# Linear attention in tiles of 64 rows by two positions, ahead of a top-2 mixture of experts, on one core

## The chip, the cores and the metric

One core of one Trainium2 chip. The metric is device time in microseconds (us), the median of several executions; lower is better. One further execution was recorded by the hardware profiler, and all rows come from it.

## What is computed

Three stages in fp32: a linear attention with a norm, a mixture of experts in which every token goes to 2 of 8 experts, and an MLP. Cut to what matters:

```python
# q, k, v: (4, 8, 576, 64)
kv = np.einsum('bhsd,bhse->bhde', k, v)
out = np.einsum('bhsd,bhde->bhse', q, kv)
x = out / sqrt(mean(out * out, -1) + 1e-6) * g_norm      # to (2304, 512)
noisy = x @ w_gate + log1p(exp(x @ w_noise)) * noise     # 8 experts
# the two largest, softmax over the two: top2, top2_w
x[t] = sum over the two e of top2_w * (relu(x[t] @ w1[e]) @ w2[e])   # 512 -> 1024 -> 512
g = s * relu(x @ w_in) ** 2 + b                          # 512 -> 2048
result = g @ w_out
```

## The kernel before, in words

The work has a front (lines 204 to 759) and a main part. The front computes the attention, the norm, the gating logits and the table that says which tokens go to which expert. The main part (from line 762) runs the experts and the MLP as a long row of matmuls (`l1`, lines 789 to 803; `l2`, lines 816 to 827), in the order written out by hand in `steps`. Engines run their instructions in program order, so a wait of one instruction holds everything behind it on that engine.

**Loads.** SyncE issues all loads of q, k and v. `load_batch` (L227) brings the first 512 of a batch's 576 positions as 128 rows of 4 positions for each of 8 heads (pieces of 1 KB), and the last 64 positions separately (`kr`, `vr`, `qr`, pieces of 256 B). Batches 0 and 1 are requested at the start, k and v of batch 2 after `kv(0)`, later ones in the loop.

**K'V.** `kv(b)` (L331) accumulates k'v of a batch: 40 fp32 matmuls with 64-column weights, 32 over 128 rows and 8 over the 64 remaining rows. An fp32 matmul stands as two records in the trace, a transpose as one. ScalarE evicts it to `kvc` and to the block-diagonal weights `kvbd`. `mfold_a` and `mfold_b` fold the gate weights in, so that one attention matmul gives output and logits.

**Token loop** (L728 to L756). There are 18 tiles of 128 tokens (`TILES`, L68): for two batches four tiles each of one position of 128 rows, and a ninth of both batches' last 64 rows. For each tile: VectorE (GpSimd from tile 10) copies q together (`repack`, L381); TensorE transposes it four times (`q_tr`, L395) and ScalarE evicts `qT`; four matmuls of 160 columns (`att`, L404; L414 for the ninth tile, in half-width weights); ScalarE evicts x (L421) and squares it (L425); VectorE copies the logits (L423) and sums the squares (L429); the inverse root goes through ScalarE (L438, L439), GpSimd (L441 to L443) and VectorE (L450); GpSimd scales the logits (L452); VectorE scales x (L461) and sums the logits (L462, `lg`); SyncE stores x to `xs` in DRAM (L467). `kv(1)` to `kv(3)` stand in the loop by `KV_AT`, their folds by `FA`, `FB`.

**Gating chain.** When the first 9 tiles have their logits, `gating(0)` (L582) starts. It is a generator that is advanced by `tick()` calls, five a tile, placed between the norm's instructions. It selects the experts (L498 to L510), ranks tokens with matmuls (L542), builds one-hots (L522, nine instructions), gets the row table of the first 256 tokens of expert 0 (`idx_e`), gathers their rows from `xs` (L186), and at its 34th tick transposes them (`put_x`, L370: L373 TensorE, L376 ScalarE, L377 VectorE). From tile 12 on `advance` splits four weight units in high and low parts (L145, L152 ScalarE, L147 VectorE, L153 GpSimd). The first expert matmul (L801) follows the last tile's attention and `put_x` on TensorE.

**End.** `finish` evicts the MLP's tiles and stores each to the rows that `out_rows` gives: one DMA of 128 rows, two for the ninth and eighteenth tile.

Of the kernel before, what the change touches and what calls it, by code (L numbers as in the profile page):

```python
# [21 lines left out]
def kernel(  # L22
# [25 lines left out]
    NP = H // 2  # L48
    NJ = 4
    SM = P * NJ  # L50
    SR = S - SM
# [13 lines left out]
    PW = 2 * HW_  # L65
# [3 lines left out]
    for b0 in range(0, B, 2):  # L69
        for b in (b0, b0 + 1):  # L70
            TILES += [(b, j) for j in range(NJ)]
        TILES.append((b0, b0 + 1, None))

    def out_rows(t):
        if len(TILES[t]) == 2:
            b, j = TILES[t]
            return [(0, P, out[b * S:b * S + SM].rearrange("(p j) d -> p j d", j=NJ)[:, j, :])]
        b0, b1, _ = TILES[t]
        return [(0, SR, out[b0 * S + SM:(b0 + 1) * S]), (SR, P, out[b1 * S + SM:(b1 + 1) * S])]
# [143 lines left out]
    def load_rest(b):  # L223
        for nm, src in (("kr", k), ("vr", v)):
            nc.sync.dma_start(KQV[b, nm], src[b, :, SM:].rearrange("h p d -> p h d"))

    def load_batch(b, what):  # L227
        def main_rows(t, src, h0, h1):
            nc.sync.dma_start(t[:, h0:h1].rearrange("p h j d -> p h (j d)"),
                              src[b, h0:h1, :SM].rearrange("h (p j) d -> p h (j d)", j=NJ))  # L230

        if what == "kv":
            for nm, src in (("k", k), ("v", v)):
                KQV[b, nm] = pool.tile([P, H, NJ, D], F32, name=nm, bufs=2)
                KQV[b, nm + "r"] = pool.tile([SR, H, D], F32, name=nm + "r", bufs=2)
            for i, (h0, h1) in enumerate(((0, H // 2), (H // 2, H)) if b == 0 else ((0, H),)):
                for nm, src in (("k", k), ("v", v)):
                    main_rows(KQV[b, nm], src, h0, h1)
                if i == 0:
                    load_rest(b)  # L240
            return
        KQV[b, "q"] = pool.tile([P, H, NJ, D], F32, name="q", bufs=2)
        for h0, h1 in ((0, H // 2), (H // 2, H)) if b == 0 else ((0, H),):
            main_rows(KQV[b, "q"], q, h0, h1)
        if b % 2 == 0:
            KQV[b // 2, "qr"] = pool.tile([P, H, D], F32, name="qr", bufs=2)
        o = SR * (b % 2)
        nc.sync.dma_start(KQV[b // 2, "qr"][o:o + SR], q[b, :, SM:].rearrange("h p d -> p h d"))

    nc.scalar.preload_act_table_set("natural_log_exp_and_others")  # L250
    for b in range(2):
        load_batch(b, "kv")
        load_batch(b, "q")
# [4 lines left out]
    def warm(n):  # L258
        ps = small_ps([P, NP, P])
        for _ in range(n):  # L260
            nc.tensor.matmul(ps, lhsT=onesb, rhs=onesb[:, None, :].to_broadcast([P, NP, P]), start=True, stop=True)
# [5 lines left out]
    gw_raw = pool.tile([P, NP, W2C], F32, name="gw_raw")  # L267
    for i, w in enumerate((w_gate, w_noise)):
        for s in range(2):
            gq.dma_start(gw_raw[s * D:(s + 1) * D, :, i * E:(i + 1) * E],  # L270
                         w.rearrange("(s n d) e -> s d n e", s=2, d=D)[s])
# [4 lines left out]
    for s in range(2):  # L276
        r = slice(s * D, (s + 1) * D)
        nc.vector.tensor_scalar(gw[r, :, s], gw_raw[r].rearrange("p (a i) c -> p a i c", a=2), gcol[r], None, op0=OP.mult)
    kvbd = []
    for b in range(B):  # L280
        t = pool.tile([P, NP, PW], F32, name=f"kvbd{b}")
        nc.gpsimd.memset(t, 0.0)
        kvbd.append(t)
    nz = gp.tile([P, NT, E], F32, name="nz")
    TB = 2 * NJ + 1
    for i in range(B // 2):
        nc.gpsimd.dma_start(nz[:, i * TB:i * TB + 2 * NJ, :].rearrange("p (b j) e -> p b (j e)", b=2),
                          noise[2 * i * S:2 * (i + 1) * S, :].rearrange("(b s) e -> b s e", b=2)[:, :SM, :]
                          .rearrange("b (p j) e -> p b (j e)", j=NJ))
    for i in range(2):  # L290
        nc.gpsimd.dma_start(nz[i * SR:(i + 1) * SR, 2 * NJ::TB, :],
                          noise.rearrange("(g b s) e -> b s g e", b=2, s=S)[i, SM:, :, :])
# [38 lines left out]
    def kv(b, h0=0, h1=H):  # L331
        K, V, KR, VR = (KQV[b, n] for n in ("k", "v", "kr", "vr"))
        ps = KVP[b] = KVP.get(b) or small_ps([P, NP, D])

        for j in range(NJ + 1):
            for h in range(h0, h1):
                hp, i = divmod(h, 2)
                lh, rh = (K[:, h, j, :], V[:, h, j, :]) if j < NJ else (KR[:, h, :], VR[:, h, :])
                nc.tensor.matmul(ps[i * D:(i + 1) * D, hp, :], lhsT=lh, rhs=rh, start=j == 0 and h - h0 < 2,
                                 stop=j == NJ and h >= h1 - 2, skip_group_check=True)  # L340
# [105 lines left out]
    def inv_end(t):  # L446
        if t < 0:
            return
# [279 lines left out]
    for t in range(NT + 1):  # L728
# [7 lines left out]
        if t:  # L736
            inv_rms(t - 1)
# [362 lines left out]
```

## Time and profile before, and how to read them

| | us |
|---|---|
| median of 3 executions | 985.84 |
| lowest, highest | 984.59, 987.8 |
| the profiled execution's own time | 983.76 |
| its span in the trace | 982.0 |
| TensorE busy (share of the span) | 942.6 (96%) |
| VectorE busy | 529.9 (54%) |
| ScalarE busy | 397.8 (41%) |
| GpSimd busy | 140.3 (14%) |

PE is TensorE's matmuls, PEld its weight loads, DVE VectorE, ACT ScalarE, POOL GpSimd, SP SyncE; a "q" behind a name is that engine's queue, where DMAs are issued. A share is an average over the whole span; what one stage is worth is read from that stage.

### The profile page before, as it was taken

To read this page: it belongs to the slowest core of one execution; us is meant where nothing else is said; L and a number is where in the kernel's file an instruction comes from. 1 tells how busy PE (TensorE), PEld (TensorE's weight loads), DVE (VectorE), ACT (ScalarE), POOL (GpSimd) and SP (SyncE) were. 2 spreads that over 40 slices of the span, in tenths; PEclk is the share of its full clock that TensorE was granted. 3 is DMA by queue.
4 is the path that set the end of the run, shared out by engine and by line. 5 is a ranking of instruction groups with operands and counts; after the bars stand their busy time and mean duration, and the time that the engine had idled before them with its cause. 6 is when DMAs were issued, how large, how long until landed. Compare 5 with 4: busy or idle time off the path is not lost.

```text
span 982.0 us, 13843 instructions
## 1 busy us (share of the span) xinstructions
PE 942.6 (96%) x5274; PEld 818.5 (83%) x5275; DVE 529.9 (54%) x979; ACT 397.8 (41%) x726; POOL 140.3 (14%) x197
## 2 busy tenths in 40 slices
PE   7866999999999999999999999999999999999998
PEld 5765878989999999999999999788788878887886
DVE  1677785544776666757546456443444443434333
ACT  2765334334554655646435443222222322222221
POOL 3566325010000100100000121100010020000000
PEclk7987999999999999999999999999999999999999
DMA  9965758445484784764645541200120020001001
GB/s 253 282 210 183 231 180 257 149 136 191 151 271 155 247 278 154 238 204 166 206 147 185 172 149 46 65 1 11 32 86 1 22 88 20 0 1 43 1 1 43
DMA packets 111849, 129.00 MB, mean 131 GB/s; under 512 B 14208, under 2 KB 80768, under 8 KB 111776
## 3 DMA queue, kind: packets, MB, share of 16 engines
q1 hardware_dynamic: 104320, 108.03, 34.2%
q0 software_dynamic: 6208, 20.00, 6.9%
q8 instruction: 42, 0.69, 0.3%
q14 instruction: 31, 0.25, 0.1%
q10 hardware_dynamic: 1248, 0.03, 0.1%
HBM read 92.91 MB, written 35.13 MB: 130 GB/s over the span
## 4 chain that ended last, share of the span: by engine, by line
PE 77%; DVE 1%; ACT 1%; issue 0%; ACTq 0%
PE ph L802 13%; PE ph L803 13%; PE ph L801 13%; PE y L825 12%; PE y L826 12%; PE y L827 12%; PE sps L373 2%; DVE r L811 0%; DVE xl L377 0%; ACT hh L813 0%; ACT r L810 0%; DVE r L812 0%; DVE hl L814 0%; DVE rows L834 0%; ACT xh L376 0%
## 5 line engine op out<-in xcount | busy, mean ns | idle before, releaser
L802 PE MATMUL ph<-xl,w1h 128*128 128x320 f32 (+3 forms) x832 | 278.4, 335 | 3.5 <-DVE xl L377 3.5
L801 PE MATMUL ph<-xh,w1h 128*128 128x320 f32 (+3 forms) x832 | 277.9, 334 | 1.5 <-DVEq L882 0.8
L803 PE MATMUL ph<-xh,w1l 128*128 128x320 f32 (+3 forms) x832 | 277.6, 334 | 0.0
L825 PE MATMUL y<-w2h,hh 128*128 128x512 f32 x608 | 243.0, 400 | 0.8 <-PEq L882 0.8
L827 PE MATMUL y<-w2h,hl 128*128 128x512 f32 x608 | 238.4, 392 | 1.0 <-DVE hl L806 1.0
L826 PE MATMUL y<-w2l,hh 128*128 128x512 f32 x608 | 238.3, 392 | 0.0
L802 PEld LDWEIGHTS ph<-xl,w1h 128*128 128x128 f32 x832 | 157.9, 190 | 19.3 <-DVE xl L377 5.9
L801 PEld LDWEIGHTS ph<-xh,w1h 128*128 128x128 f32 x832 | 158.0, 190 | 17.6 <-ACT xh L376 2.3
L803 PEld LDWEIGHTS ph<-xh,w1l 128*128 128x128 f32 x832 | 157.9, 190 | 9.8
L805 ACT ACTIVATE hh<-ph 128x320 fp32r<-128x320 f32 (+2 forms) x128 | 55.9, 437 | 227.0 <-PE ph L803 227.0
L811 DVE SCALAR_TENSOR_TENSOR r<-ph,r 128x512 f32<-128x512 f32 (+1 forms) x80 | 51.0, 638 | 175.9 <-ACT r L810 175.6
L806 DVE SCALAR_TENSOR_TENSOR hl<-ph,hh 128x320 fp32r<-128x320 f32 (+2 forms) x128 | 62.4, 489 | 141.5 <-ACT hh L805 141.5
L827 PEld LDWEIGHTS y<-w2h,hl 128*128 128x128 f32 x608 | 114.4, 188 | 26.4 <-DVE hl L806 1.5
L825 PEld LDWEIGHTS y<-w2h,hh 128*128 128x128 f32 x608 | 114.7, 189 | 21.9 <-ACT xh L376 1.1
L826 PEld LDWEIGHTS y<-w2l,hh 128*128 128x128 f32 x608 | 114.7, 189 | 20.3
L810 ACT ACTIVATE r<-ph 128x512 f32<-128x512 f32 (+1 forms) x80 | 44.4, 554 | 187.8 <-PE ph L803 187.8
L813 ACT ACTIVATE hh<-r 128x512 fp32r<-128x512 f32 (+1 forms) x80 | 47.1, 589 | 101.5 <-DVE r L812 101.5
L186 POOL DMA_INDIRECT rows<-xs,idx x35 | 34.8, 996 | 314.1 <-PE sps L373 183.6
L814 DVE TENSOR_TENSOR hl<-r,hh 128x512 fp32r<-128x512 f32 (+1 forms) x80 | 51.1, 639 | 52.5 <-ACT hh L813 52.5
L186 POOL DMA_INDIRECT rows<-ys,slot_i x36 | 34.5, 959 | 268.3 <-DVE rows L783 133.0
L147 DVE SCALAR_TENSOR_TENSOR w1l<-raw,gcol,w1h 128x512 fp32r<-128x512 f32 x64 | 50.7, 793 | 22.3 <-ACT w1h L145 17.6
L152 ACT ACTIVATE w2h<-raw 128x512 fp32r<-128x512 f32 x80 | 49.7, 621 | 1.5 <-DMA raw<-in_moe_w_dram 1.2
(170 smaller groups left out, 838.9 us busy)
## 6 DMA issues: line engine op xcount, KB each, us to landing
raw<-in_moe_w_dram SPq DMA_DIRECT2D x128, 256.0 KB, 3.7
ys<-rows SPq DMA_DIRECT2D x40, 256.0 KB, 3.7
c_raw<-in_moe_w_in_dram SPq DMA_DIRECT2D x16, 512.0 KB, 6.1
c_raw<-in_moe_w_out_dram SPq DMA_DIRECT2D x16, 512.0 KB, 7.9
wd<-c_fl SPq DMA_DIRECT2D x16, 512.0 KB, 4.8
raw<-wd SPq DMA_DIRECT2D x32, 256.0 KB, 2.9
ys<-zero SPq DMA_DIRECT2D x13, 512.0 KB, 5.5
xs<-x SPq DMA_DIRECT2D x18, 256.0 KB, 5.0
```

Source lines behind the costliest of these rows:

```text
L147: nc.vector.scalar_tensor_tensor(l1.rearrange(fl), r1.rearrange(fl), gcol, h1.bitcast(F32).rearrange(fl), op0=OP.mult, op1=OP.subtract)
L186: nc.gpsimd.indirect_dma_start(out=dst, out_offset=None, in_=src, in_offset=bass.IndirectOffsetOnAxis(ap=icol, axis=0))
L801: nc.tensor.matmul(ps[:, :wd], lhsT=w1h[:, c, :], rhs=xh[:, c, cs], start=c == 0, stop=False)
L802: nc.tensor.matmul(ps[:, :wd], lhsT=w1h[:, c, :], rhs=xl[:, c, cs], start=False, stop=False)
L803: nc.tensor.matmul(ps[:, :wd], lhsT=w1l[:, c, :], rhs=xh[:, c, cs], start=False, stop=c == KC - 1)
L805: nc.scalar.activation(hh[:, cs], ps[:, :wd], AF.Relu)
L806: nc.vector.scalar_tensor_tensor(hl[:, cs], ps[:, :wd], 0.0, hh[:, cs].bitcast(F32), op0=OP.max, op1=OP.subtract)
L811: nc.vector.scalar_tensor_tensor(r[:, :wd], ps[:, :wd], 0.0, r[:, :wd], op0=OP.max, op1=OP.mult)
L814: nc.vector.tensor_sub(hl[:, cs], r[:, :wd], hh[:, cs].bitcast(F32))
L825: nc.tensor.matmul(y, lhsT=hh[:, cs], rhs=w2h, start=f == 0, stop=False)
L826: nc.tensor.matmul(y, lhsT=hh[:, cs], rhs=w2l, start=False, stop=False)
L827: nc.tensor.matmul(y, lhsT=hl[:, cs], rhs=w2h, start=False, stop=f == nf - 1)
```

## The change

Tiles become 64 rows (`HP`) by two positions (`NJ` = 9 positions a row): tile i of a batch is positions 2i and 2i+1 for the same 64 rows, and the ninth tile holds position 8 of both batches. The last 64 positions are no longer special.

- **Loads**: q, k and v of a batch are read flat, as 4 blocks `m` of 128 rows with 576 floats each (pieces of 2304 B). Rows 0 to 63 of block m are head 2m, rows 64 to 127 head 2m+1. q has three buffers.
- **kv**: K is 64 rows and 64 columns, so each matmul uses a quarter of the array: 9 positions x 4 blocks x 2 heads = 72 matmuls a batch, into two accumulators. ScalarE evicts one half of `kvc`, VectorE the other; the block-diagonal copies are split likewise (`kv_diag`, `mfold_b`). `kv(1)`, `kv(2)`, `kv(3)` stand whole behind tile 2, 6 and 11.
- **q_tr**: no repacking; 8 plain matmuls with the identity, 64-column weights straight from q, two tiles ahead. `qT` of odd tiles is evicted by VectorE.
- **att**: 8 matmuls with 64-column weights and 160 columns.
- **Norm**: two tiles a step (`CHUNKS`). One eviction of all 640 columns a tile by ScalarE; squares, sums, Ln, Exp and the scaling are done for both tiles at once; what GpSimd did of it goes to VectorE. One store for two tiles.
- **Noise**: two loads and six copies on GpSimd in place of four loads.
- **Output**: every tile is stored by two DMAs of 64 rows.

The ticks become nine for two tiles; the 34th falls behind the last tile's attention, in the norm of tiles 15 and 16.

```diff
-    NP = H // 2
-    NJ = 4
-    SM = P * NJ
-    SR = S - SM
+    HP = P // 2
+    NJ = S // HP
+    NM = H // 2
...
-            TILES += [(b, j) for j in range(NJ)]
-        TILES.append((b0, b0 + 1, None))
+            TILES += [((b, j), (b, j + 1)) for j in range(0, NJ - 1, 2)]
+        TILES.append(((b0, NJ - 1), (b0 + 1, NJ - 1)))
...
+    def load(b, nm, m0=0, m1=NM):
+        src = {"q": q, "k": k, "v": v}[nm][b].rearrange("h s d -> (h s d)").rearrange("(m r x) -> r m x", r=P, x=NJ * D)
+        if m0 == 0:
+            KQV[b, nm] = pool.tile([P, NM, NJ, D], F32, name=nm, bufs=3 if nm == "q" else 2)
+        nc.sync.dma_start(KQV[b, nm].rearrange("p m j d -> p m (j d)")[:, m0:m1], src[:, m0:m1])
...
+        for j in range(NJ):
+            for a in range(a0, a1):
+                for m in range(2):
+                    for i in range(2):
+                        r = slice(i * HP, (i + 1) * HP)
+                        nc.tensor.matmul(ps[i][m * D:(m + 1) * D, a, :], lhsT=K[r, 2 * a + m, j, :], rhs=V[r, 2 * a + m, j, :],
+                                         start=j == 0 and a == a0, stop=j == NJ - 1 and a == a1 - 1, skip_group_check=True)
+        if a1 == 2:
+            KVP[b] = kvc = pool.tile([P, 2, 2, D], F32, name="kvc", bufs=1)
+            nc.scalar.activation(kvc[:, :, 0], ps[0], AF.Copy)
+            nc.vector.tensor_copy(kvc[:, :, 1], ps[1])
...
+    def q_tr(t):
+        pt = small_ps([P, 2, 2, P])
+        for i, (b, j) in enumerate(TILES[t]):
+            for a in range(2):
+                for m in range(2):
+                    nc.tensor.matmul(pt[m * D:(m + 1) * D, i, a, :], lhsT=KQV[b, "q"][:, 2 * a + m, j, :], rhs=ident,
+                                     start=True, stop=True)
+        qT = pool.tile([P, 2, 2, P], F32, name="qT", bufs=3)
+        if t % 2:
+            nc.vector.tensor_copy(qT, pt)
...
+    def squares(c):
+        x, = XC[c]
+        n = CHUNKS[c][1]
+        sq = pool.tile([P, 2, H, D], F32, name="sq", bufs=1)
+        nc.scalar.activation(sq[:, :n], x[:, :n, :, :D], AF.Square)
...
+        nc.vector.tensor_reduce(ss[:, :n], sq[:, :n], axis=AX, op=OP.add)
...
+    def norm(c):
...
+        nc.vector.tensor_scalar(ss, ss, -0.5 / D, -0.5e-6, op0=OP.mult, op1=OP.add)
+        nc.vector.tensor_mul(u, y, y)
+        tick()
+        nc.vector.tensor_mul(u, u, ss)
+        nc.vector.scalar_tensor_tensor(y, u, 1.5, y, op0=OP.add, op1=OP.mult)
+        tick()
+        nc.vector.tensor_mul(x[:, :, :, D:], x[:, :, :, D:], y[:, :, :, None].to_broadcast([P, n, H, W2C]))
+        tick()
+        nc.vector.tensor_reduce(lg[:, t0:t0 + n, :], x[:, :, :, D:].rearrange("p n h c -> p n c h"), axis=AX, op=OP.add)
+        tick()
+        xn = pool.tile([P, 2, H, D], F32, name="xn", bufs=3)[:, :n]
+        nc.vector.tensor_mul(xn, x[:, :, :, :D], y[:, :, :, None].to_broadcast([P, n, H, D]))
+        tick()
...
+    KV_AT = {2: 1, 6: 2, 11: 3}
+    LOADS = {3: (3, "kv"), 8: (3, "q")}
+
+    for c, (t0, n) in enumerate(CHUNKS):
+        for i in range(n):
+            t = t0 + i
+            att(t)
+            if t - 1 in KV_AT:
+                mfold_a(KV_AT[t - 1])
+            if t + 2 < NT:
+                q_tr(t + 2)
+            if t - 1 in KV_AT:
+                mfold_b(KV_AT[t - 1])
+            if c and i == 0:
+                inv_rms(c - 1)
+            evict(c, i)
+            if t in KV_AT:
+                kv(KV_AT[t])
+            if t in LOADS:
+                b, nms = LOADS[t]
+                for nm in nms:
+                    load(b, nm)
+            if c and i == n - 1:
+                norm(c - 1)
+            if 12 <= t < 16:
+                advance(t - 11)
+            elif t == 11:
+                advance(0)
+        if c and CHUNKS[c - 1][0] + CHUNKS[c - 1][1] == NT0:
             chain[:] = [gating(0), 0]
+        squares(c)
+        put_rows()
```

## Rows read from the trace of the kernel before

**Rows 1.** Timeline, TensorE: start us, us, engine, line, instruction; first expert matmul.

```profile
87.83 0.58 PE L801 MATMUL ph<-xh,w1h 128*128 128x256 f32 x1
```

**Rows 2.** Busy time of TensorE by stretches from 87.83 to 982, their sum.

```profile
sum 894.17, PE 880.09; mean PE 73.34
```

**Rows 3.** Busy us (x) of PE, PEld, DVE, ACT, POOL; PEclk, DMA share, GB/s.

```profile
30.00:40.00 10.00, 6.80 (x76) 6.14 (x77) 8.70 (x23) 7.60 (x21) 5.70 (x13) 1.00 1.14 285
...
60.00:70.00 10.00, 4.50 (x31) 4.33 (x30) 9.62 (x26) 4.42 (x12) 6.81 (x13) 0.77 0.49 166
...
80.00:90.00 10.00, 5.83 (x29) 4.59 (x30) 8.18 (x17) 6.00 (x13) 7.60 (x15) 0.50 0.71 221
```

**Rows 4.** The same view in stretches of 2 us during the loads.

```profile
20.00:22.00 2.00, 2.00 (x9) 1.85 (x8) 0.00 (x0) 0.98 (x3) 0.00 (x0) 0.50 1.10 350
...
22.00:24.00 2.00, 2.00 (x10) 1.96 (x10) 0.29 (x1) 0.92 (x2) 0.00 (x0) 0.50 1.27 212
```

**Rows 5.** Timeline, VectorE: waits for q, first normalization; [idle before <-releaser].

```profile
17.50 1.10 DVE L387 COPY qc<-q 128x512 f32<-128x512 f32 x3 [5.78 <-DMA q<-in_q_dram]
...
30.06 0.43 DVE L387 COPY qc<-q 128x512 f32<-128x512 f32 x1 [5.03 <-DMA q<-in_q_dram]
...
31.38 0.69 DVE L461 TENSOR_TENSOR x<-x,iv 128x512 f32<-128x512 f32 x1
```

**Rows 6.** Timeline, TensorE: K'V, attention of tile 0, quarter weights, half-width attention.

```profile
12.88 1.98 PE L339 MATMUL sps<-v,k 128*64 128x64 f32 x32 [0.76 <-DMA v<-in_v_dram]
...
20.56 2.45 PE L410 MATMUL att<-kvbd,qT 128*128 128x160 f32 x8
...
39.88 0.31 PEld L339 LDWEIGHTS sps<-vr,kr 64*64 64x64 f32 x8
...
45.73 1.31 PE L414 MATMUL att<-kvbd,qT 128*64 128x160 f32 x16
```

**Rows 7.** Groups by shape, 0 to 200 us: count | busy us, mean ns | idle before.

```profile
L429 DVE TENSOR_REDUCE ss<-sq 128x8 f32<-128x512 f32 x18 | 12.2, 677 | 1.4 <-ACT sq L425 1.4
...
L461 DVE TENSOR_TENSOR x<-x,iv 128x512 f32<-128x512 f32 x18 | 12.4, 688 | 0.4
...
L462 DVE TENSOR_REDUCE lg<-raw 128x16 f32<-128x128 f32 x18 | 6.6, 367 | 6.2 <-POOL raw L452 6.2
...
L450 DVE SCALAR_TENSOR_TENSOR iv<-iu,iv 128x8 f32<-128x8 f32 x18 | 3.0, 164 | 4.5 <-POOL iu L443 4.5
...
L498 DVE TENSOR_REDUCE m_all<-g 128x9 f32<-128x72 f32 x4 | 0.9, 229 | 1.4 <-POOL g L485 1.3
...
L834 DVE COPY rows<-y 128x512 f32<-128x512 f32 x2 | 1.4, 682 | 0.0
...
L421 ACT ACTIVATE x<-att 128x512 f32<-128x512 f32 x18 | 10.5, 582 | 3.5 <-PE att L410 3.5
...
L425 ACT ACTIVATE sq<-x 128x512 f32<-128x512 f32 x18 | 11.3, 630 | 0.6
...
L438 ACT ACTIVATE iv<-ss,eps 128x8 f32<-128x8 f32 x18 | 5.4, 299 | 13.0 <-DVE iv L450 10.5 <-DVE ss L429 2.3
...
L145 ACT ACTIVATE w1h<-raw,gcol 128x512 fp32r<-128x512 f32 x21 | 15.1, 717 | 9.2 <-DMA raw<-in_moe_w_dram 9.0
```

**Rows 8.** Timeline, second half of the front, all engines.

```profile
55.05 0.26 ACT L481 ACTIVATE g<-lg 128x72 f32<-128x72 f32 x1 [0.24 <-DVE lg L462]
...
68.36 3.61 DVE L522 TENSOR_SCALAR ohe<-io,early 128x256 f16<-128x256 f16 x9
...
72.77 0.74 DVE L147 SCALAR_TENSOR_TENSOR w1l<-raw,gcol,w1h 128x512 fp32r<-128x512 f32 x1
...
78.50 1.25 POOL L186 DMA_INDIRECT rows<-xs,idx_e  x1 [0.75 <-DVE iv L450]
...
83.60 1.97 PE L373 MATMUL sps<-ident,rows 128*128 128x128 f32 x8 [3.63 <-DMA rows<-xs,idx_e]
```

**Rows 9.** Timeline, SyncE's queue at the end of the kernel.

```profile
977.90 1.11 SPq L842 DMA_DIRECT2D out_dram<-rows  x2
```

More of the change, by code (lines that the diff above doesn't have):

```diff
@@ L221 @@
     KQV = {}
[L223 to L248, printed above, removed]
-    nc.scalar.preload_act_table_set("natural_log_exp_and_others")
-    for b in range(2):
-        load_batch(b, "kv")
-        load_batch(b, "q")
+    def load(b, nm, m0=0, m1=NM):
[3 more added lines that the diff above has]
+        nc.sync.dma_start(KQV[b, nm].rearrange("p m j d -> p m (j d)")[:, m0:m1], src[:, m0:m1])
+    nc.scalar.preload_act_table_set("natural_log_exp_and_others")
+    for m0 in range(0, NM, NM // 2):
+        for nm in "kv":
+            load(0, nm, m0, m0 + NM // 2)
+    load(0, "q")
+    for nm in "kvq":
+        load(1, nm)
     onesb = gp.tile([P, P], BF16, name="onesb")
@@ L258, in warm @@
     def warm(n):
-        ps = small_ps([P, NP, P])
+        ps = small_ps([P, KC, P])
         for _ in range(n):
-            nc.tensor.matmul(ps, lhsT=onesb, rhs=onesb[:, None, :].to_broadcast([P, NP, P]), start=True, stop=True)
+            nc.tensor.matmul(ps, lhsT=onesb, rhs=onesb[:, None, :].to_broadcast([P, KC, P]), start=True, stop=True)
     warm(14)
@@ L266 @@
     gq = nc.scalar
-    gw_raw = pool.tile([P, NP, W2C], F32, name="gw_raw")
+    gw_raw = pool.tile([P, NM, W2C], F32, name="gw_raw")
     for i, w in enumerate((w_gate, w_noise)):
-        for s in range(2):
-            gq.dma_start(gw_raw[s * D:(s + 1) * D, :, i * E:(i + 1) * E],
-                         w.rearrange("(s n d) e -> s d n e", s=2, d=D)[s])
+        gq.dma_start(gw_raw[:, :, i * E:(i + 1) * E], w.rearrange("(m r) e -> r m e", r=P))
     for i in range(2):
@@ L402, in q_tr @@
         QT[t] = qT
     def att(t):
-        tl = TILES[t]
         qT = QT.pop(t)
-        ps = fps.tile([P, NP, 256], F32, name="att", bufs=2)
-        for hp in range(NP):
-            if len(tl) == 2:
-                nc.tensor.matmul(ps[:, hp, :PW], lhsT=qT[:, hp, :], rhs=kvbd[tl[0]][:, hp, :], start=True, stop=True)
-            else:
-                for i in range(2):
-                    r = slice(i * SR, (i + 1) * SR)
-                    nc.tensor.matmul(ps[r, hp, :PW], lhsT=qT[:, hp, r], rhs=kvbd[tl[i]][:, hp, :],
-                                     start=True, stop=True)
@@ L465, in put_rows @@
-    def put_rows():
-        t, x = XO.pop(0)
-        nc.sync.dma_start(xs[t * P:(t + 1) * P, :], x)
+        ps = fps.tile([P, 2, 512], F32, name="att", bufs=2)
+        pv = ps[:, :, :H // 2 * HW_].rearrange("p a (m i c) -> p a m i c", m=2, i=2)
+        for a in range(2):
+            for i in range(2):
+                for s_, (b, _) in enumerate(TILES[t]):
+                    r = slice(s_ * HP, (s_ + 1) * HP)
+                    nc.tensor.matmul(pv[r, a, :, i, :], lhsT=qT[:, s_, a, i * HP:(i + 1) * HP], rhs=kvbd[b][:, a, i],
+                                     start=True, stop=True)
@@ L470, with put_rows @@
+    def put_rows():
+        if not XO:
+            return
+        t, n, x = XO.pop(0)
+        nc.sync.dma_start(xs[t * P:(t + n) * P, :].rearrange("(n p) d -> p n d", n=n), x.rearrange("p n h d -> p n (h d)"))
     GT = {}
```

206 lines of the change are left out of this document (71 added, 135 removed).

## The prediction

> **What bounds the kernel now.** I first looked for the point from which TensorE doesn't rest. The timeline shows the first expert matmul at 87.83 us [rows 1]; from there to the end TensorE is busy 880.09 of 894.17 us [rows 2]. The change leaves that part alone except for the last stores. So the time is the start of that matmul plus a nearly fixed 894 us, and only the front, 0 to 88 us, has to be worked out. 1 us there is 1 us of the result.
>
> In the front I read busy time by stretches [rows 3]. From 30 to 40 us VectorE is the fullest engine (8.70 of 10 us), from 60 to 70 it is full (9.62) while TensorE has 4.50, and TensorE runs at the lower of its two clocks (0.50, 1.2 GHz) from 80 to 90. The DMA share is 1.14 at 285 GB/s in the loading time. There the rate swings between 350 and 212 GB/s in stretches of 2 us with the share never under 1.1 [rows 4]: the engines are always occupied, and the slow stretches are those in which the 256 B pieces of the last 64 positions come. VectorE waits twice for q, 5.78 and 5.03 us [rows 5]. So the front is bound by loads to 30 us, then by VectorE together with what holds it up: waits for GpSimd of 6.2 us before the logit sums and 4.5 us before the roots [rows 7].
>
> **The loads.** 14.2 MB come in pieces of 2304 B instead of 1 KB and 256 B. I take 350 GB/s, the better row [rows 4]; the bounds are 285 [rows 3] and no loss. Batch 0's k and v (2.36 MB) then land at 12.4 us instead of before the matmul at 12.88 [rows 6]; q of batch 1, 4.72 MB later, at 12.4 + 13.5 = 25.9, where before it held VectorE to 30.06 [rows 5]: 4 us earlier.
>
> **K'V.** 72 matmuls instead of 40 a batch, 144 records instead of 80. At the low clock 32 records took 1.98 us [rows 6], 62 ns each, so 31 ns at full clock: 144 x 31 = 4.5 us. If the four quarters overlap fully it is half, 2.2. The eight records on quarter weights took 0.31 us [rows 6], 39 ns each, which is no gain by size and 5.6 us for 144. Bounds 2.2 and 5.6, and I take 3.7, the side of the rows. For batch 0 only the second half (72 records) follows the last landing, at the low clock: 72 x 62 ns = 4.4 us against 2.5 for 40 records. Counting 0.5 us earlier landing, 1.9 us more K'V, and q already there (it came at 17.50 [rows 5], by my reckoning 1.2 us after TensorE could have used it), the first attention matmul is at about 20.8 instead of 20.56 [rows 6]. What lies ahead of it stays: GpSimd's six noise copies push its constants, and VectorE's that hang on them, back by some 4 us, to about 15, hidden by K'V's end at 16.8. Uncovered they would cost up to 4.
>
> **TensorE's tile.** Sixteen half-width records of 160 columns took 1.31 us [rows 6]: that is att, 1.1 us pitch without its tail. q_tr is 16 records of 128 columns, 0.9. Together 2.0 a tile: by themselves no bound.
>
> **VectorE's step of two tiles.** Removed: repacking, the logit copies, half of the instruction starts. Added: evicting qT of the odd tile (0.68, as L834), three small instructions from GpSimd and the logit scaling. From 72 to 512 columns a sum grows from 229 to 677 ns, 1.0 ns a column [rows 7], so 1024 columns cost 1.2. A step is then 0.68 + 1.2 (sums of squares) + 4 x 0.16 + 0.42 (logits) + 0.50 (their sums) + 1.2 (x) = 4.7 us, and its norm alone 2.8. ScalarE: 0.6 (qT) + 2 x 0.7 (eviction, 640 columns) + 1.05 (squares) + 0.6 (Ln, Exp) = 3.6 [rows 7]. Instructions alone, this is no slower than 31.38 to 55.05 us now [rows 5, 8], 2.6 us a tile.
>
> **The wait that is added.** `kv(b)`, its folds and their copies stand between a step's first and second tile, and VectorE now takes part in them. In its order the kvc copy, the diagonal copy, qT and the folded weights come ahead of the norm of the step before. So that norm waits for TensorE: K'V 3.7, then att 1.1, fold 0.4, q_tr 0.9, fold 0.55, copy 0.25: 3.2 more. Queued behind it are norm, sums, then Ln on ScalarE, the eviction, the next attention.
> - First time: att(0) at 20.8, four more pieces of 1.0 to 1.1 to 25.9, q_tr(4) to 26.8 (q has landed), kv(1) to 30.5, norm(0) at 33.7 instead of 31.38. Norm 2.8, sums 1.2, Ln and Exp 0.6: norm(1) 38.3 to 41.1, sums to 42.3.
> - Second: eviction of tile 4 by 39.0, att(6) and q_tr(8) to 41.0, kv(2) to 44.7, norm(2) at 47.9; sums to 51.9, norm(3) 52.5 to 55.3, tile 8's sums to 56.0. The first 9 tiles' logits are there at about 58, against 55.05 [rows 8].
> - Third: sums of tiles 9, 10 end at 60.9; tile 9's eviction at 57.3, att(11), q_tr(13) to 59.3, kv(3) to 63.0, norm(5) at 66.2: about 4 us in which VectorE has little to do.
>
> **The gating half.** norm(5) 2.8 + twelve selections of 0.23 + a weight low part 0.74 + sums 1.2 = 7.5: 73.7. Then `advance(2)` puts a low part ahead of norm(6); it waits for Ln, Exp, an eviction and the high part on ScalarE (0.6 + 0.7 + 0.72 = 2.0), then 0.74 + 2.8 + 0.5 (ranks) + 3.6 (one-hots) + 0.74 + 1.2: 85.3. Again 2.0 + 0.74 and 0.14 for `idx_e`: 88.2. From the gather to the transposes of the gathered rows takes 5.1 us (78.50 to 83.60 [rows 8]): 93.3. Transposes at the low clock 2.0, the eviction 0.6: first expert matmul at 95.9, 8.1 us later than now [rows 1]. What VectorE still owes after it (about 5 us) is as much as before, so no gain or loss there.
>
> **The end.** Three more stores among the last four tiles; two stores of one tile take 1.11 us in the queue [rows 9], one every 0.5 us. They wait mostly for evictions: 0.2, bounds 0 and 1.5.
>
> **Sum.** +8.1 + 0.2 = +8.3 us on the profiled execution's 983.76, which lies 2.1 under the median. Carried over to the median: 985.84 + 8.3, about 994.
>
> **Rivals.**
> - *Quarters side by side.* With 2.2 us a K'V the three norms behind it start 1.5 us earlier each (4.5), batch 0's half 2.2 us: 994 - 6.7 = 987.4, no change that can be told. For it: different rows and columns of the array share nothing. Against: quarter weights show 39 ns a record, not 16 [rows 6]. The Trainium skill, TensorEngine Tiling (Array Packing), Key Properties, says that tiles operate independently and load weights and multiply in parallel, and counts four of them in the 64x64 mode; that is this rival, and no run here shows four. Chance 0.17.
> - *Faster: the waits go and nothing takes their place.* Its place is VectorE's queue. The 4.1 us of earlier q (30.06 to 25.9) come through whole, and the waits for GpSimd, 6.2 and 4.5 us [rows 7], vanish, less about 4 us of added work: 4.1 + 6.7 = 10.8 at most, 975; with half of it handed on, 980.5. It decides if norm(0) starts before about 30 us, that is, if TensorE gets through K'V and folds while VectorE still has sums to do. For it: the full DMA share [rows 3]. Against: the order of the instructions. Chance 0.23.
> - *Low clock in the loop.* If TensorE is granted 1.2 GHz there as at 80 to 90 us [rows 3], K'V and what follows cost 3 to 4 us more each time: 994 + 9 = 1003. Chance 0.08, as TensorE is fuller than before in the first half.
> - The change does not do what it says: it does it in every tile; left out.
>
> **How the numbers follow.** The forecast has 0.52. About 0.3% (3 us) is what a measurement of this kernel can tell from no change. Slower: 0.52 and 0.08, with a little of the forecast's spread (K'V at 2.9, one-hots without GpSimd beside them at 2.2) in the middle: 0.59. Same 0.18, faster 0.23. The forecast's own range is 988 to 999. The range asked for reaches down into the faster rival, 981 to 999.
>
> **What would show it.** Right: k and v of batch 0 land at 12 to 12.5 us with DMA near 350 GB/s; K'V of 144 records near 3.7 us; VectorE idle before norm at about 28 to 33, 43 to 47 and 61 to 66 us, released by TensorE; first L801 record near 96; 894 us behind it. Wrong: VectorE over 9 tenths busy from 30 us on, or the first expert matmul before 85 us; K'V near 2.2 us makes the first rival right; a PEclk of 0.5 between 30 and 65 us the third.

## The result and the profile after

The changed kernel takes 994.98 us in the median of 4 runs (993.61 to 997.58), the kernel before 985.53 on the same chip (4 runs; the 985.84 of the table is the median of three of them): a ratio of 1.0096, 95% interval [1.0069, 1.0123]. The profiled execution took 993.61 us with a span of 991.9, 9.85 us more than the one before.

TensorE's timeline of the changed kernel (start us, us, engine, line, instruction, [idle before <-releaser]) answers to [rows 1, 6]:

```profile
10.96 2.05 PE L322 MATMUL sps<-v,k 64*64 64x64 f32 x72 [1.90 <-DMA v<-in_v_dram]
...
18.56 1.25 PE L397 MATMUL att<-kvbd,qT 128*64 128x160 f32 x16
...
24.19 1.09 PE L380 MATMUL sps<-ident,q 128*64 128x128 f32 x16 [0.46 <-DMA q<-in_q_dram]
...
25.22 2.33 PE L322 MATMUL sps<-v,k 64*64 64x64 f32 x144
...
31.96 0.55 PE L354 MATMUL sps<-gw,kvT 128*128 128x64 f32 x4 [1.78 <-issue]
...
40.42 2.33 PE L322 MATMUL sps<-v,k 64*64 64x64 f32 x144
...
58.77 2.40 PE L322 MATMUL sps<-v,k 64*64 64x64 f32 x144
...
95.32 0.58 PE L789 MATMUL ph<-xh,w1h 128*128 128x256 f32 x1 [0.69 <-ACT xh L370]
```

The first attention matmul comes 2.0 us earlier than before, q of tile 4 (batch 1) has landed at 24.2, and a K'V product of 144 records takes 2.33 to 2.40 us. All of that is better than before or than forecast, and yet the first expert matmul comes at 95.32, 7.5 us later than in [rows 1]. Behind it the row of matmuls is nearly what it was [rows 2]; here is its sum, and the last stores in SyncE's queue [rows 9]:

```profile
sum 896.58, PE 881.43; mean PE 881.43
...
983.95 4.96 SPq L830 DMA_DIRECT2D out_dram<-rows  x8
```

896.58 us in place of 894.17. From the first of the last stores to the end of the span it is now 991.9 - 983.95 = 7.95 us; before, that store was issued at 975.74, 6.26 us from the end. So of the 9.9 us of span 7.5 arose in the front, 1.7 at the end and 0.7 in between.

Stretches of the front: busy us (count) of PE, PEld, DVE, ACT, POOL; PEclk, DMA share, GB/s, as in [rows 3, 4]:

```profile
20.00:30.00 10.00, 9.54 (x256) 8.55 (x252) 2.49 (x4) 5.40 (x11) 0.00 (x0) 1.00 1.06 391
...
30.00:40.00 10.00, 6.56 (x99) 6.22 (x97) 7.32 (x18) 5.22 (x9) 0.00 (x0) 1.00 0.93 345
...
60.00:70.00 10.00, 8.53 (x178) 7.54 (x169) 6.29 (x22) 5.54 (x12) 1.42 (x2) 1.00 0.34 107
...
80.00:90.00 10.00, 5.50 (x44) 3.95 (x44) 8.60 (x17) 3.89 (x7) 2.96 (x3) 0.50 0.46 154
```

From 20 to 30 us the loads run at 391 GB/s, above the better row of before (350), and TensorE is full at its upper clock. VectorE, which was full from 60 to 70 [rows 3], now has 6.29 of 10 us there, and GpSimd has nearly nothing to do. So VectorE, the engine that was short of time, now has time to spare there, and yet the front ends later. Its timeline shows where it waits:

```profile
27.64 0.29 DVE L327 COPY kvc<-sps 128x128 f32<-128x128 f32 x1 [2.77 <-PE sps L322]
...
28.03 0.29 DVE L337 COPY kvbd<-kvc 64x256 f32<-64x256 f32 x1
...
30.22 0.69 DVE L384 COPY qT<-sps 128x512 f32<-128x512 f32 x1 [1.90 <-PE sps L380]
...
32.79 0.23 DVE L360 COPY kvbd<-sps 64x64 f32<-64x64 f32 x1 [1.88 <-ACT kvbd L358]
...
33.05 0.17 DVE L439 TENSOR_SCALAR ss<-ss 128x16 f32<-128x16 f32 x1
```

Between the sum of squares that ends at 24.87 and the first instruction of norm(0) at 33.05 (L439) VectorE works 1.5 us (0.29 + 0.29 + 0.69 + 0.23) and waits the rest, each time for a piece of the K'V product or its folds, or for query transposes. Only then does the norm get its turn, which needs none of them. In ScalarE's timeline the same kind of wait stands at 72.83:

```profile
66.26 1.05 ACT L418 ACTIVATE sq<-x 128x1024 f32<-128x1024 f32 x1
...
72.83 0.31 ACT L429 ACTIVATE iv<-ss,eps 128x16 f32<-128x16 f32 x1 [5.51 <-DVE ss L421]
...
73.29 0.68 ACT L411 ACTIVATE x<-att 128x640 f32<-128x640 f32 x1
```

The two instructions of the inverse root (L429 and the one behind it) wait 5.51 us for VectorE's sum, and the eviction at 73.29, on which TensorE's next attention hangs, waits behind them. Over the front it is 24.6 us in 9 places.

In the last stretch of the front VectorE hands over the row table `idx_e`, and TensorE then waits for the gathered rows:

```profile
86.67 0.15 DVE L523 TENSOR_SCALAR idx_e<-sps 128x2 int32<-128x2 f32 x1
...
91.88 1.12 PE L367 MATMUL sps<-ident,rows 128*128 128x128 f32 x4 [4.06 <-DMA rows<-xs,idx_e]
```

### The profile page after: what moved, and what is told of

The parts are those of the page before. It is cut to its first block, busy times and chain, and to the rows that moved or that the text cites. A ratio compares the mean times of both kernels' runs of the same rounds, so it can differ in the third digit from the quotient of the medians.

```text
span 991.9 us, 14894 instructions
## 1 busy us (share of the span) xinstructions
PE 950.9 (96%) x5874; PEld 822.8 (83%) x5875; DVE 534.1 (54%) x981; ACT 386.8 (39%) x685; POOL 107.2 (11%) x122
## 4 chain that ended last, share of the span: by engine, by line
PE 76%; DVE 1%; ACT 1%; issue 0%; ACTq 0%
PE ph L790 13%; PE ph L791 13%; PE ph L789 12%; PE y L813 12%; PE y L814 12%; PE y L815 12%; PE sps L367 2%; DVE r L799 0%; ACT hh L801 0%; ACT r L798 0%; DVE xl L371 0%; DVE r L800 0%; DVE hl L802 0%; DVE rows L822 0%; ACT xh L370 0%
## 5 line engine op out<-in xcount | busy, mean ns | idle before, releaser
L794 DVE SCALAR_TENSOR_TENSOR hl<-ph,hh 128x320 fp32r<-128x320 f32 (+2 forms) x128 | 62.5, 490 | 142.3 <-ACT hh L793 136.2
L801 ACT ACTIVATE hh<-r 128x512 fp32r<-128x512 f32 (+1 forms) x80 | 47.1, 589 | 101.8 <-DVE r L800 97.9
L143 DVE SCALAR_TENSOR_TENSOR w1l<-raw,gcol,w1h 128x512 fp32r<-128x512 f32 x64 | 47.8, 748 | 24.5 <-ACT w1h L141 19.9
```

Source lines behind the costliest of these rows:

```text
L794: nc.vector.scalar_tensor_tensor(hl[:, cs], ps[:, :wd], 0.0, hh[:, cs].bitcast(F32), op0=OP.max, op1=OP.subtract)
```

## The experiments

Each kernel is the changed one with one edit or several; a ratio is always to the kernel before, run on the same chip, so the changed kernel's 1.0096 is the figure to hold it against. The changed kernel itself was not run again on those chips, so where two intervals overlap the two ratios are not told apart. A single trace has a spread too: in the two runs below that leave the front alone and change only stores (one store a tile, half of the stores on ScalarE) the first expert matmul comes at 96.12 and 97.24 us, beside 95.32 in the changed kernel. A difference of under 2 us at this one instruction shows nothing.

**Norm ahead of K'V.**

```diff
             evict(c, i)
+            if c and i == 0 and t in KV_AT:
+                norm(c - 1)
             if t in KV_AT:
                 kv(KV_AT[t])
...
-            if c and i == n - 1:
+            if c and i == n - 1 and t0 not in KV_AT:
```

> The edit: in the three steps that hold a K'V product of a later batch, the norm of the step before is issued ahead of that product and its folds, everything else as in the changed kernel. Theory (VectorE's norm stands behind K'V and its folds: 5.5, 4.7 and 4.2 us between the end of the K'V product and the first norm instruction, at 33.05, 47.40 and 65.35 us): the first expert matmul moves from 95.3 to 89.5-93 us, the norms of these steps start 3 us earlier or more, and the whole time falls by 2.5 to 6 us to 989-992.5. Rival (VectorE's own work or the place of the ticks sets the end of the front, and the wait is made good later): the norms start earlier but the first expert matmul stays within 1 us of 95.3, time 994-995.

Ratio 1.0103 [1.0082, 1.0125]. norm(0) and norm(2) moved to 26.2 and 42.1 us, as wanted, but the first expert matmul is no earlier: 97.68, against 95.32 to 97.24 with the front of the changed kernel. VectorE's folded copies show what was paid for it:

```profile
49.28 0.23 DVE L360 COPY kvbd<-sps 64x64 f32<-64x64 f32 x1 [0.59 <-ACT kvbd L358]
...
97.68 0.58 PE L791 MATMUL ph<-xh,w1h 128*128 128x256 f32 x1 [0.69 <-ACT xh L370]
```

The second fold, at 47.1 in the changed kernel, is ready at 49.28, and the third at 71.3 in place of 64.7. In a queue that is worked in order the norm and the folds only change places. TensorE then waits 5.5 us in 3 places, from 15 to 100 us, for VectorE's copy of the K'V product (L327), for which it had no wait in that stretch of the changed kernel. My theory fell. The rival's outcome (norms earlier, first expert matmul and time as they were) agrees with the ratio and is not told apart from a small loss by this one trace.

**Row halves outermost in K'V.**

```diff
-        for j in range(NJ):
-            for a in range(a0, a1):
-                for m in range(2):
-                    for i in range(2):
+        for i in range(2):
+            for j in range(NJ):
+                for a in range(a0, a1):
+                    for m in range(2):
```

> The edit: in the K'V product the row half becomes the outermost loop, so that two neighbouring matmuls share their rows of the array and only the column half alternates; same number of matmuls. Theory (16 ns a matmul comes from neighbours that lie in different row and column quarters and run side by side): a K'V product of 144 matmuls takes 3.4-5.6 us in place of 2.33, the norms behind it start 1 to 3 us later, and the whole time is 1 to 6 us longer (995.5-1001). Rival (a small matmul of 36 columns takes 16 ns anyway, in whatever order): 2.3 us, norms and time as in the changed kernel, 994-995.5.

```profile
27.33 4.24 PE L322 MATMUL sps<-v,k 64*64 64x64 f32 x144
...
42.71 4.24 PE L322 MATMUL sps<-v,k 64*64 64x64 f32 x144
...
62.08 4.24 PE L322 MATMUL sps<-v,k 64*64 64x64 f32 x144
...
100.34 0.58 PE L789 MATMUL ph<-xh,w1h 128*128 128x256 f32 x1 [0.69 <-ACT xh L370]
```

The same 144 records take 4.24 us in place of 2.33, 29 ns each in place of 16, by their order alone. That is what the theory says (a record has 64 columns, not the 36 that the expectation names). One rival is left: the row half also decides to which of the two accumulators a matmul adds, so neighbours that share their rows now share their accumulator too, and this run does not tell the two apart. The first expert matmul comes at 100.34, 3.1 to 5.0 us later, for 3 x 1.9 us. The ratio is 1.0125 [1.0103, 1.0146], about 0.3% over the changed kernel's with overlapping intervals; from the first expert matmul to the end it is 893.8 us in place of 896.6.

**One store a tile.**

```diff
-                for p0, p1, ap in out_rows(b0 + i):
-                    nc.sync.dma_start(ap, yo[p0:p1])
+                nc.sync.dma_start(out_rows(b0 + i), yo)
```

Here `out_rows` gives one access pattern of 2 halves, 64 rows and 512 floats.

> The edit: an output tile is stored by one DMA that covers both its halves, in place of two DMAs of 64 rows. Theory (the last 1.7 us of the loss come from twice as many stores, issued one after the other behind the last output copy): from the last output copy to the end of the span 4.0-4.4 us in place of 5.8, first expert matmul unchanged at 95.3, time 992.8-993.8. Rival (the end is set by the landing of the last pieces, whose number is unchanged): 5.5-6 us at the end, time 994.5-995.5.

Ratio 1.0214 [1.0193, 1.0236]: a miss on both sides. SyncE's queue at the end, then the DMA engines' busy tenths and GB/s from 975 to 1003 us in 40 slices of 0.7 us:

```profile
982.50 7.93 SPq L831 DMA_DIRECT2D out_dram<-rows  x4
...
DMA  0000000000000111111111366311111111111000
...
GB/s 0 0 0 0 0 0 0 0 0 0 0 0 18 29 23 29 44 50 50 53 53 50 73 214 170 67 59 53 53 50 50 53 53 50 50 53 50 6 0 0
```

Four stores of 256 KB end 20 us after the first is issued, for most of it at 50 to 53 GB/s with one tenth of the 16 DMA engines busy; the eight stores of the changed kernel reached about 200 GB/s. The Trainium skill, "DMA: Bandwidth & Descriptors", section "Why a DMA increments its semaphore by 16 and not by 1", has the rule: a DMA runs on the largest number of engines, up to 16, that divides the slowest dimension of its access patterns; with a slowest dimension of 2 that is two engines. The trace agrees but for the short stretch at up to 214 GB/s, which I have not traced to a store. About the end's 1.7 us this run says nothing.

**Two ticks an evicted tile** (in `evict`).

```diff
         tick()
+        tick()
```

> The edit: an evicted tile advances the gating chain by two stages in place of one, so that the indices and the token rows of the last step are asked for earlier; the arithmetic is the same. Theory (VectorE's work in order, with the norms late behind the folds, sets the front's end): the first expert matmul moves by at most 1 us either way, since the same VectorE work is ahead of it, and the time stays at 993.5-996. Rival (the loss comes from where the gating stages stand, fewer steps for as many stages): first expert matmul 5 to 8 us earlier (87.5-90.5), time 987-990.

Ratio 1.0076 [1.0059, 1.0094], some 0.2% less than the changed kernel's, with overlapping intervals. The first expert matmul comes at 89.09, so the rival is right about the front, with VectorE's norms no earlier (norm(5) at 65.99 in place of 65.35). But the first store of an expert's block comes at 125.82, against 128.00 in the changed kernel and 120.82 before: of the 6.2 us gained, 4 are lost again in between. The first expert matmul, and ScalarE's timeline, which shows to what:

```profile
89.09 0.58 PE L790 MATMUL ph<-xh,w1h 128*128 128x256 f32 x1
...
91.01 0.31 ACT L430 ACTIVATE iv<-ss,eps 128x16 f32<-128x16 f32 x1 [3.55 <-DVE ss L422]
...
95.19 0.30 ACT L430 ACTIVATE iv<-ss,eps 128x8 f32<-128x8 f32 x1 [2.36 <-DVE ss L422]
...
95.64 0.64 ACT L794 ACTIVATE hh<-ph 128x256 fp32r<-128x256 f32 x2
```

The copy of the first hidden block (L794) stands behind the inverse root of the last tile, which waits for VectorE's sum. TensorE waits 2.8 us for that copy.

**Fold copies on ScalarE.**

```diff
-            nc.vector.tensor_copy(kvc[:, :, 1], ps[1])
+            nc.scalar.activation(kvc[:, :, 1], ps[1], AF.Copy)
...
-                nc.vector.tensor_copy(dst, kvc[r])
+                nc.scalar.activation(dst, kvc[r], AF.Copy)
...
-                nc.vector.tensor_copy(kvbd[b][r, :, :, m, D:], pm[r, :, m])
+                nc.scalar.activation(kvbd[b][r, :, :, m, D:], pm[r, :, m], AF.Copy)
```

> The edit: the copies of K'V, of its diagonal and of the folded gate weights that stood on VectorE go to ScalarE; nothing else moves. Putting the norm ahead of the K'V product brought the norms forward (26.2 and 42.1 us in place of 33.0 and 47.4) and the folds back, and the first expert matmul came 2.4 us later: the two only change places in VectorE's queue. Theory (VectorE's queue stands still for the round trip TensorE, ScalarE, TensorE, ScalarE of each fold, with the norm behind it): without the folds in it the norms of these steps start at 29-31, 44-46 and 62-64 us in place of 33.0, 47.4 and 65.4, the first expert matmul comes 1.5-4 us earlier (91.5-94), time 991.5-994. Rival (the round trip itself, through TensorE's order, sets the steps): norms within 1 us of where they are or moved by ScalarE's longer queue, first expert matmul 94.5-97, time 994-996.5.

Ratio 1.0050 [1.0032, 1.0068]: half of the loss is gone, with 12 small copies moved. The first expert matmul comes at 91.37 (PE), norm(5) at 60.79 in place of 65.35 (DVE):

```profile
91.37 0.58 PE L789 MATMUL ph<-xh,w1h 128*128 128x256 f32 x1 [0.69 <-ACT xh L370]
...
30.39 0.69 DVE L384 COPY qT<-sps 128x512 f32<-128x512 f32 x1 [4.79 <-PE sps L380]
...
31.00 0.16 DVE L439 TENSOR_SCALAR ss<-ss 128x16 f32<-128x16 f32 x1
...
46.65 0.69 DVE L384 COPY qT<-sps 128x512 f32<-128x512 f32 x1 [3.08 <-PE sps L380]
...
47.26 0.16 DVE L439 TENSOR_SCALAR ss<-ss 128x16 f32<-128x16 f32 x1
...
60.79 0.17 DVE L439 TENSOR_SCALAR ss<-ss 128x16 f32<-128x16 f32 x1
```

The theory holds for the sum and for the third step. What had been won in the first step is not kept: norm(3) starts at 51.63, in the changed kernel at 51.79. In the second step norm(2) stays at 47.26, because the wait behind which it stands is now another: the query transposes of an odd tile (L384), 3.08 us there, 4.79 ahead of norm(0), and 19.6 us in 5 places over the front.

**Second half of the fold behind the norm.** The call of `mfold_b` moves behind `norm(c - 1)` of its step, and its VectorE copy goes to ScalarE.

```diff
-            if t - 1 in KV_AT:
-                mfold_b(KV_AT[t - 1])
             if c and i == 0:
                 inv_rms(c - 1)
...
                 norm(c - 1)
+            if t - 1 in KV_AT:
+                mfold_b(KV_AT[t - 1])
```

> The edit: the second half of the fold (the product with the gate weights and its two copies, now both on ScalarE) is issued behind the norm of its step, instead of between the query transposes and the eviction. Theory (what holds the steps with a K'V product is that norm, eviction and query transposes of the same step stand behind the fold's round trip, while the folded weights are not needed before the next tile of another batch, one to two tiles on): norms of these steps 2-4 us earlier, attention of the next batch not later than now by more than 1.5 us, first expert matmul 2-5 us earlier (90.5-93.5), time 990-993. Rival (whoever is moved back takes the place of the one moved forward, as with the norm): first expert matmul 94.5-98, time 994-997.

Ratio 1.0069 [1.0055, 1.0083], first expert matmul at 92.53. Norms at 31.6, 47.7 and 62.7. The gain is of the theory's size, but no larger than with all the copies off VectorE and the fold in its place (the intervals overlap, and so do the first expert matmuls within the spread), so the later place of the fold is not shown to help.

**Half of the output stores on ScalarE.**

```diff
-                    nc.sync.dma_start(ap, yo[p0:p1])
+                    (nc.scalar if p0 else nc.sync).dma_start(ap, yo[p0:p1])
```

> The edit: of the two stores of an output tile the second is issued by ScalarE in place of SyncE. Theory (the end grew by 1.7 us because eight stores are issued one after the other at 0.62 us): from the last output copy to the end 4.0-4.8 us in place of 5.8; the time 993-994 (1-1.7 us less). Rival (the landing of the last piece of 64 rows sets the end, from whichever queue): 5.5-6 us, time as the changed kernel. The single store of both halves was no answer to that: its pieces went at 50 GB/s, where the eight stores reach 200 GB/s.

Ratio 1.0087 [1.0068, 1.0106], not to be told from 1.0096. From the first of the last stores to the end it is 996.7 - 989.72 = 6.98 us in place of 7.95: 1.0 of the 1.7 us, in between the two expectations, as ScalarE issues two stores in 1.38 us and makes its own last copy only after that.

**Late fold, all fold copies on ScalarE, two ticks, half of the stores on ScalarE**, together:

> The edits together: fold issued behind the norm with all its copies on ScalarE, two ticks an evicted tile, second half of the output stores on ScalarE. Theory (three separate losses: the fold's wait, the place of the gating stages, the end): the gains add up, -2 to -4 by the fold, -3.4 as measured by the ticks, -1 to -1.7 at the end: time 985.5-989, first expert matmul 84.5-88. Rival (behind the front VectorE has the work of the later token tiles left over in any case, so that an earlier first expert matmul is given back): first expert matmul 85-89, the first store of an expert's block at 124 us or later as with the ticks alone (125.8), time 989-992.

Ratio 1.0028 [1.0014, 1.0041], first expert matmul at 86.79, first store of an expert's block at 124.50. What the rival says of the place is borne out, as with the ticks alone: TensorE waits 3.2 us for ScalarE's copy of the first hidden block, which again stands behind an inverse root that waits 2.36 us for VectorE.

**Inverse root behind the eviction.**

```diff
-            if c and i == 0:
-                inv_rms(c - 1)
             evict(c, i)
+            if c and i == 0:
+                inv_rms(c - 1)
```

> The edit: the two ScalarE instructions of the inverse norm of the step before are issued behind the first eviction of a step, instead of ahead of it; nothing else moves. Theory (ScalarE's queue stands still in front of that eviction: in the changed kernel it waits 24.6 us in 9 places for VectorE's sum of squares, and TensorE's next attention waits for the eviction, 9.4 us in 5 places): ScalarE's wait for the sum falls below 12 us, TensorE's wait for evictions below 5 us, the first expert matmul comes 1.5-5 us earlier (90.3-93.8), time 990-993.5. Rival (VectorE's own work, 8.4 to 8.7 us of every 10 from 70 us on, sets the front's end): the evictions come earlier, the first expert matmul stays within 1 us of 95.3, time 993.5-996.

Ratio 1.0093 [1.0075, 1.0111], first expert matmul at 96.47. Of the theory's two waits one fell and one did not. Waits of ScalarE and of TensorE from 15 to 100 us (waited for: us in total, times, longest):

```profile
ACT iv L429 <- DVE ss L421: 21.3, 8, 5.4
...
PE att L397 <- DVE qT L384: 4.0, 2, 2.2
...
PE att L397 <- DVE iu L440: 3.4, 1, 3.4
```

ScalarE still waits 21.3 us for the sums. TensorE's wait for evictions, 9.4 us in the changed kernel, is gone from its list, and its attention then waits for VectorE instead, for `qT` and for the norm's own small instructions. The first expert matmul is no earlier and the time the same: the rival's outcome. Its reason, VectorE's own work, is not ruled out: VectorE is busy 9.22 of 10 us from 70 to 80 and 9.19 from 80 to 90. Alone, this edit is worth nothing.

**Fold copies and all query evictions on ScalarE, inverse root behind the eviction.** The two edits above and, for the queries:

```diff
-        if t % 2:
-            nc.vector.tensor_copy(qT, pt)
-        else:
-            nc.scalar.activation(qT, pt, AF.Copy)
+        nc.scalar.activation(qT, pt, AF.Copy)
```

> The edits together: fold copies on ScalarE (measured alone: first expert matmul at 91.4, time 0.46% less than the changed kernel's), inverse norm behind the first eviction, all query transposes evicted by ScalarE. With the folds gone VectorE still stood 19.6 us in 5 places waiting for query transposes of odd tiles, with norms and sums of squares queued behind them. Theory (the loss is head-of-queue waiting of VectorE and ScalarE for each other and for TensorE, not work): first expert matmul 86-90, time 984.5-989. Rival (from 55 us on VectorE is busy 8 to 9 us of 10 in the order of the gating stages, so waits removed early are made up later): first expert matmul 90-92.5, time 989.5-992.5.

Ratio 1.0013 [0.9998, 1.0028]: the time of the kernel before. VectorE's first three norms, TensorE's first expert matmul, and the sum behind it:

```profile
27.83 0.17 DVE L436 TENSOR_SCALAR ss<-ss 128x16 f32<-128x16 f32 x1 [0.37 <-ACT iv L426]
...
38.67 0.17 DVE L436 TENSOR_SCALAR ss<-ss 128x16 f32<-128x16 f32 x1 [2.26 <-ACT iv L426]
...
43.25 0.17 DVE L436 TENSOR_SCALAR ss<-ss 128x16 f32<-128x16 f32 x1 [0.37 <-ACT iv L426]
...
88.38 0.58 PE L786 MATMUL ph<-xh,w1h 128*128 128x256 f32 x1 [0.69 <-ACT xh L370]
...
sum 894.82, PE 880.79; mean PE 880.79
```

norm(0) starts 5.2 us earlier than in the changed kernel, norm(2) 4.2 us. The first expert matmul comes 6.9 us earlier, and this time it is kept: the first store of an expert's block is at 120.56, before at 120.82. But the two early norms are not where it is won. Here are norm(3), VectorE's last folded copy and norm(5) of the changed kernel, then norm(3) and norm(5) of this one:

```profile
51.79 0.17 DVE L439 TENSOR_SCALAR ss<-ss 128x16 f32<-128x16 f32 x1 [0.38 <-ACT iv L429]
...
64.67 0.23 DVE L360 COPY kvbd<-sps 64x64 f32<-64x64 f32 x1 [2.74 <-ACT kvbd L358]
...
65.35 0.17 DVE L439 TENSOR_SCALAR ss<-ss 128x16 f32<-128x16 f32 x1
...
51.77 0.18 DVE L436 TENSOR_SCALAR ss<-ss 128x16 f32<-128x16 f32 x1 [0.38 <-ACT iv L426]
...
60.01 0.17 DVE L436 TENSOR_SCALAR ss<-ss 128x16 f32<-128x16 f32 x1
```

At norm(3) both kernels are at the same place; from there to norm(5) it is 13.6 us in the changed kernel and 8.2 in this one (13.5 in the two runs that change only stores, 8.2 in the next version below). So 5.3 of the 6.9 us are won at the third K'V product. In that stretch VectorE has 3.4 us less waiting and 2.0 us less work, the copies themselves. The arithmetic and the tiles are those of the changed kernel. No run takes the work away and leaves the waits, or the other way round, and how much of the step from 91.37 to 88.38 is due to the queries and how much to the inverse root was not run apart.

**The same, with the last tile's two stores on ScalarE, and that with two ticks as well.**

```diff
-                    nc.sync.dma_start(ap, yo[p0:p1])
+                    (nc.scalar if g == NG - 1 and i == nb - 1 else nc.sync).dma_start(ap, yo[p0:p1])
```

> The edits together: fold copies and all query evictions on ScalarE, inverse norm behind the first eviction (measured together at the time of the kernel before, 1.0013), and, new, the two stores of the very last output tile issued by ScalarE; SyncE keeps six. Theory (of the end's 1.7 us the queue of issues at 0.62 us each makes up at least 1 us): from the first of the last stores to the end 6.5-7.2 us in place of 8, all else as without it; time 0.1% less, 983.0-985.0, 0.998 to 1.0015 of the kernel before. Rival (as with half of all stores on ScalarE, 1.38 us for two issues there give most of it back): 7.5-8 us at the end, ratio 1.001 to 1.0025.

> The same with two ticks an evicted tile. Theory (the inverse norm of the last tile stands ahead of the first unit's ScalarE copy and waits for VectorE, so that an earlier first expert matmul is mostly given back before the first block of an expert is stored; with the ticks alone 6.2 us were gained at the first matmul and 2.2 at the first store): first expert matmul 82-85, first store at 118.5-120.5 in place of 120.6, time 981.5-984. Rival (with the waits gone the gating stages are no longer in the way, and two ticks only push the norms back): first expert matmul 85-88, first store 120.5-123, time no less than the version beside it.

Ratios 1.0018 [1.0002, 1.0035] and 1.0006 [0.9988, 1.0024]. From the first of the last stores to the end the first of them has 982.5 - 975.29 = 7.21 us in place of 7.89 without the edit: 0.7 us, less than the runs can tell. With two ticks the first expert matmul comes at 85.11, earlier than in the kernel before, and the first store of an expert's block at 121.58, later than there:

```profile
91.50 0.30 ACT L427 ACTIVATE iv<-ss,eps 128x8 f32<-128x8 f32 x1 [3.12 <-DVE ss L419]
...
91.95 0.64 ACT L791 ACTIVATE hh<-ph 128x256 fp32r<-128x256 f32 x2
```

Again the hidden block's copy stands behind an inverse root that waits 3.12 us. No version is shown to beat the kernel before.

## Why the prediction was right or wrong, point by point

**The whole and the front.** Forecast 994.0, measured 994.98. The front was forecast 8.1 us longer, and is 7.5. The mechanism, that VectorE's norm stands behind the K'V product and its folds in the order of instructions, is borne out by the fold copies on ScalarE (-4.0 us at the first expert matmul) and by the three edits together (-6.9 us). It was put too narrowly, though. Moving the norm ahead did not help, since whatever is queued last pays; what helped was to take the copies that wait off VectorE's queue. The query evictions, which the forecast counted only as 0.68 us of work, wait too (19.6 us in 5 places once the folds are gone), but they were not moved alone. It was also put too widely: only the wait at the third K'V product is shown to cost time at the end; what was won at the first two was gone by norm(3). And the forecast took the place of the gating stages as given: two ticks a tile bring the first expert matmul 6.2 us forward with the norms where they were, though only 2.2 us of it reach the first store.

**The gating half.** It came as forecast: from norm(5) to the end of the tile sums 7.5 us forecast and 7.4 measured (65.35 to 72.79), to the next 11.6 and 11.4 (to 84.18), the row table at 88.2 and 86.67, from there to the transposes 5.1 and 5.2. Only the transposes and their evictions take 3.4 us in place of 2.6. Two errors cancel inside it: the nine one-hots take 2.88 us in place of 3.6, and one 0.17 us instruction of norm(6) takes 1.25.

**Loads.** Taken at 350 GB/s with batch 1's q at 25.9; it came at 391, and q by 24.2. The first attention matmul, forecast at 20.8, came at 18.56, more by the K'V product than by the loads: batch 0's second half, put at 4.4 us, takes 2.05.

**K'V: mis-sized.** 3.7 us taken "on the side of the rows", with bounds 2.2 and 5.6; it takes 2.33. The step that failed is the weight I gave to the 39 ns of the eight quarter-weight records [rows 6]: those are weight loads, not matmuls, and all lie on one row half and alternate in columns only. The kernel with row halves outermost shows 29 ns for such neighbours at the upper clock and 16 when rows (and accumulators) alternate. So the premise of the rival with quarters side by side, that a K'V product takes near 2.2 us, is right, and its time of 987.4 is not, since the wait behind the product was longer.

**The wait behind K'V: mis-sized the other way.** 3.2 us from the end of the K'V product to the norm was forecast. It is 5.5, 4.7 and 4.2 us (27.55 to 33.05, 42.75 to 47.40, 61.17 to 65.35). Left out of the sum were, the first time, 1.78 us in which TensorE's own queue supplied nothing (L354, "issue"), the second time 0.41 us of the same in the attention; each time ScalarE's copy of the folded weights, 0.25 us, for which VectorE's own copy waits (L358, L360); and the third time two instructions of the selection ahead of the norm, 0.42 us. The rest is in pieces that took a little longer than I had put down. The two errors nearly cancel: the norms were forecast at 33.7, 47.9 and 66.2. A good landing of the total is thus in part luck: it hides two terms off by a third and more.

**Faster, the waits going and nothing taking their place.** Its point of decision was a norm(0) before about 30 us; it came at 33.05. In the kernel with three edits it is at 27.83, and the time is still not that rival's 980.5 but that of before. The waits for GpSimd of [rows 7] did go. What holds that kernel from 70 us on is open: VectorE is busy 8.59 of 10 us from 70 to 80 and 9.01 from 80 to 90 there, which speaks for its work, but no run took work from it in that stretch.

**Low clock.** Not in the loop: PEclk is 1.00 in every 10 us from 20 to 70 us, 0.50 from 80 to 90 as before [rows 3].

**The end: out of its bounds.** 0.2 us with bounds 0 and 1.5; it is 1.7. "They wait mostly for evictions" was wrong: eight stores go out back to back, 4.96 us of issuing at 0.62 us each, longer than the evictions take (the last output copy ends 2.1 us after the first of these stores is issued). ScalarE as second issuer gets 0.7 to 1.0 us back. What the rest is stays open.

## What to carry to other kernels

Where an engine works its queue in order, ask of every instruction given to it what it waits for, and not only how long it takes: moving twelve copies of 0.2 to 0.3 us and nine of 0.7 off VectorE (with the inverse root behind the eviction, which alone was worth nothing) brought the first expert matmul 6.9 us forward. Moving the waiting instruction to another engine helped; swapping it with its neighbour did not. Ask also at which step the gain is kept: two of the three waits here could go without anything to show for it at norm(3). And an earlier start of the next stage counts only if that stage's own first copies don't stand behind the old one's last: follow it to the first output, not to the first matmul.

## What was not expected of the hardware

- Quarter-array matmuls of 64 columns take 16 ns a record when neighbours alternate in rows and columns of the array (144 in 2.33 us), and 29 ns when only the columns alternate (144 in 4.24 us). With the rows the accumulator alternates too; which of them does it is not shown.
- After the first fast K'V product TensorE's queue ran dry: 1.78 us marked "issue" in the changed kernel, 1.65 to 1.87 in nine of the others, 0.69 with the norm ahead; none in the kernel whose K'V takes 4.24 us, and none in the one with late fold, two ticks and half of the stores together, where the same matmul waits 1.6 us for ScalarE. So part of the faster product may have been given back there. The cause was not tried.
- Small VectorE instructions that otherwise take 0.17 to 0.23 us took 1.34, 1.25 and 1.18 us at 66.47, 75.28 and 86.74 in the changed kernel, each time as a subtraction of 128x512 on GpSimd had just begun (66.44, 75.17 and 86.57). That is 3.2 us of VectorE's time in the stretch that ends in the gather of the rows; no run took one of them away.
- Stores whose slowest dimension is 2 moved 50 to 53 GB/s; the same tiles as stores of 64 rows each took 8 us in all, in place of 20.
- Loads in pieces of 2304 B ran at 383 to 401 GB/s in stretches of 2 us from 12 to 30 us, where the pieces of 1 KB and 256 B had 350 and 212 [rows 4].
